# Attention into an ELU layer on one core: two tiles of tokens share each first product from tile 8 on, and the second products run some ten steps behind

## The chip, the cores and the metric

The kernel runs on one core of one Trainium2 chip. A core has a matrix engine (TensorE, PE in the profile), a vector engine (VectorE, DVE), a scalar engine (ScalarE, ACT), a GpSimd engine (POOL) and a sync engine (SP). Each has its own queue of instructions. SP, ACT and POOL also issue DMA transfers, which all run on the same 16 DMA engines. SBUF is the working memory, with 128 partitions; PSUM is the memory that TensorE writes, in eight banks of 128 partitions by 2 KB. The metric is the device time of one execution in microseconds (us), less being better.

## The reference

```python
def _attn_ref(q, k, v):                       # 8 batches, 8 heads, 576 positions, 64 numbers
    scores = scale * np.matmul(q, k.transpose(0, 1, 3, 2))
    mask = np.abs(pos[:, None] - pos[None, :]) <= 32
    scores = np.where(mask, scores, -1000000000.0)
    ...softmax over the last axis...
    return np.matmul(attn, v)

x = attn_out.transpose(0, 2, 1, 3).reshape(4608, 512)
h = x @ w_in                                  # 512 x 2048
g = np.where(h > 0.0, h, np.exp(np.minimum(h, 0.0)) - 1.0)
out = g @ w_out                               # 2048 x 512
```

So a sliding-window attention makes 4608 tokens of 512 numbers each, and a two-layer network with an ELU between its layers turns them into the output. All inputs and the output are float32.

## The kernel before

**Tokens.** The 4608 tokens are cut into 18 tiles of 256 tokens (`TT`), numbered t. Attention works on blocks of 64 positions and takes two blocks at a time, a pair i of 128 tokens; there are 36 pairs, and tile t consists of pairs 2t and 2t+1. A batch is nine blocks, that is four and a half pairs.

**Steps.** The network's work is cut into 144 steps, kk, in the order of the list `order`. A step is one tile and two of the sixteen 128-wide blocks of the inner layer (`FG` = 2), so a tile has eight steps. Steps 0 to 15 are those of tiles 0 and 1 mixed; from step 16 on tile t has steps 8t to 8t+7. In a step:

- `mm1` makes the first products of the step into a PSUM bank (`h0` and `h1` in turn): eight matmuls of a 128x128 block of `w_in` with 256 columns of `xT`, the tile's attention output turned to feature rows (L728).
- `exponents` takes the exponential of the bank on ACT (L738), `subtract` takes 1 from it on DVE (L750), and `elu` combines that with the bank on DVE into `g_sb` (L761). `elu` of step kk is queued in step kk+1. Since there are two banks, the first products of step kk+2 can start only when `elu` of step kk has read its bank.
- `mm2` adds the second products of step kk-2 (`LAG` = 2) to the tile's sums `psY` in PSUM banks `y0` and `y1`: four matmuls with 512 columns (L773). After a tile's last step ACT copies one half of the sums out and DVE the other (`y_sb`, L290 and L292), and SP issues two output DMAs of 256 KB. The next tile's sums start in the same two banks.

**Attention between the steps.** The rest is put at steps by hand: `at(kk, slot, fn, ...)` queues a call at a slot of step kk. Within a step come, in this order, `elu` of the step before, the slot "dve", the first products with their exponential and subtraction, the slot "mid", the second products with their copies, and the slot "end". `begin[i]` is the step at which pair i starts, and both pairs of a tile start together: scores of both (L384) at "mid" of step S = `begin[i]`, exponentials `pu` of 1024 columns on ACT at S and S+1 (L395), masks `pm` on DVE at S+1 and S+2 (L404), the products with v at the end of S+2 (L416), and `normalize` into `x_st` on DVE at S+3 and S+4 (L425, L428). From pair 10 on `x_dma` then turns `x_st` into `xT` by a transposing DMA from SP (L455), at the ends of S+3 and S+4. `x_st` has two buffers, so that a pair's `normalize` waits for the transposing DMA of the pair two before it.

**Loading a batch.** For batches 3 to 7, q and k are loaded in float32 by four DMAs of 576 KB from SP (`load_qk`, L132, at step `l_qk`), cast in six parts to bf16 (`cast_qk`), written as rows to DRAM from the ACT queue (`write_rows`, L319), and read back by two transposing DMAs from SP (`transpose_rows`, L324). v is loaded by five DMAs from POOL (`load_v`, L151, from step `l_v`), and a copy of it shifted by 64 rows is made, on DVE (`rotate_v`, L175) or for batches 2 and 3 by DMA from SP (`rotate_v_dma`, L183). The steps of all this are in the table `{2: (0, 0, 0), 3: (15, 24, 22), ...}` at L642, whose third number is where the casts may begin.

The instructions of each engine run in the order in which the program makes these calls. The functions that the change touches, with the lines of the profile:

Of the kernel before, what the change touches and what calls it, by code (L numbers as in the profile page):

```python
# [21 lines left out]
def kernel(  # L22
# [100 lines left out]
    def load_qk(b, which, part, engs=(nc.sync, nc.sync)):  # L123
        z, nj = part
        mj = max(nj, HJ)
        t = lpool.tile([128, 2, mj * D], FP32, tag=f"f{which}{mj}",
                       name=f"f{which}", bufs=2 if part is WHOLE else 1)
        qk_f[b, which, z] = t
        src = (q, k)[which][b, :, z:z + NC * nj, :].rearrange(
            "(g h) (c j) d -> c g h (j d)", h=2, j=nj)  # L130
        for h in range(2):
            engs[h].dma_start(out=t[:, h, 0:nj * D], in_=src[:, :, h, :])  # L132
# [161 lines left out]
    def cast_qk(b, which, part, j0, n, eng, hs=slice(0, 2)):  # L294
        z, nj = part
        if (b, which, z) not in qk_b:
            qk_b[b, which, z] = lpool.tile(
                [128, max(nj, HJ), 2 * D], BF16,
                tag=f"b{which}{max(nj, HJ)}", name="qkb",
                bufs=2 if part is WHOLE else 1)  # L300
        t = qk_b[b, which, z]
        copy_on(eng,
                t[:, j0:j0 + n, :].rearrange("p j (h d) -> p h j d",
                                             h=2)[:, hs],
                qk_f[b, which, z][:, hs, j0 * D:(j0 + n) * D].rearrange(
                    "p h (j d) -> p h j d", d=D))
# [136 lines left out]

    def xT_of(i):
        t, z = i // 2, i % 2
        if z == 0:
            xT[t] = xpool.tile([128, 2, NDO, 128], BF16, tag="xT", name="xT")
        return xT[t][:, z, :, :]
# [168 lines left out]
    begin = {4: 9, 5: 12, 6: 18, 8: 26, 10: 31, 12: 37}  # L617
    for i in range(FIRST_TWO, NPAIR):
        begin[i] = begin.get(i - i % 2, STEPS * (i // 2) - 14)
# [15 lines left out]
    at(BACK_AT, "dve", swap_back)  # L635
    starts = set(begin.values())
    starts |= {begin[i] + 1 for i in range(FIRST_TWO, NPAIR)}
    for b in range(2, B):
# [3 lines left out]
        l_qk, l_v, c0 = {2: (0, 0, 0), 3: (15, 24, 22), 4: (35, 36, 41),  # L642
                         5: (52, 52, 57), 6: (68, 68, 73),
                         7: (84, 84, 89)}[b]
# [7 lines left out]
        if b <= 3:  # L652

            if b == 2:
                at(k0, "dve", rotate_v, b, 0, 1)
            at((21, 28)[b - 2], "mid", rotate_v_dma, b, 3 - b)
        else:
            for n, back in enumerate((10, 8, 3, 2)):
                m0 = 2 * (n // 2)
                at(k0 - back, "dve", rotate_v, b, m0, m0 + 2, (n % 2,))  # L660
# [12 lines left out]
        for n, (which, j0) in enumerate(  # L673
# [3 lines left out]
            if j0 == 12:  # L677
                at(free[n], "end", write_rows, b, which)
                at(free[n] + (3 if free[n] == 29 else 4), "mid",
                   transpose_rows, b, which)  # L680

    order = [(z, n + m) for n in range(0, HALF, 2) for z in range(2)
             for m in range(2)]
    order += [(z, n) for n in range(HALF, STEPS) for z in range(2)]
    order += [(t, n) for t in range(2, NT) for n in range(STEPS)]
    psH, e_t, m_t, g_t, psY = {}, {}, {}, {}, {}

    def mm1(kk):  # L690
        t, s = order[kk]
        if kk == BY_PAIRS[1]:
            return
        ks = BY_PAIRS if kk == BY_PAIRS[0] else (kk,)
        tags = ((f"h{kk % 2}", "s") if kk == NSTEP - 1 else
                ("s",) if kk == 2 else ("u",) if kk == 3 else (f"h{kk % 2}",))
# [6 lines left out]
        for p in range(len(ks)):  # L703
            for k in ks:
                for z in range(len(tags)):
                    products(k, z, p if len(ks) > 1 else None)
                if p == len(ks) - 1:
                    for z in range(len(tags)):
                        exponents(k, z)
                        if k == NSTEP - 1:  # L710
                            elu(k, z)
# [4 lines left out]
    def products(kk, z, pair):  # L716
        t, s = order[kk]
        ps = psH[kk][z]
        w = ps.shape[1]
        for j in range(w):  # L720
# [32 lines left out]
    def elu(kk, z=0):  # L753
        if z == 0:
            g_t[kk] = mpool.tile([128, FG, TT], BF16, tag="g_sb", name="g_sb",
                                   bufs=6)
# [10 lines left out]
    def sums_to(kk, ts, j, c):  # L767
        t, s = order[kk]
        to, cs = psY[t][ts], slice(0, D_MODEL)
        if c is not None:  # L770
            cs = slice(c * D_MODEL // 2, (c + 1) * D_MODEL // 2)
            to = psY[t][ts + c][:, 0:D_MODEL // 2]
        nc.tensor.matmul(  # L773
            to,
            lhsT=g_t[kk][:, j, ts * 128:(ts + 1) * 128],
            rhs=w_out_sb[:, s * FG + j, cs],
            start=(s == 0 and j == 0),
            stop=(s == STEPS - 1 and j == FG - 1))

    def rows_out(ts, c, eng):  # L780
        t = NT - 1
        if c is None:
            src, cs = psY[t][ts], slice(0, D_MODEL)
        else:
            cs = slice(c * D_MODEL // 2, (c + 1) * D_MODEL // 2)
            src = psY[t][ts + c][:, 0:D_MODEL // 2]
        y_sb = opool.tile([128, D_MODEL], FP32,
                          tag=f"y_sb{int(eng is nc.vector)}", name="y_sb")
        copy_on(eng, y_sb[:, cs], src)
        (nc.scalar if c == 1 else nc.sync).dma_start(  # L790
            out_t[t, :, ts, cs], y_sb[:, cs])

    def mm2(kk, parts=((0, 0), (0, 1), (1, 0), (1, 1))):
        t, s = order[kk]
        if s == 0:
            psY[t] = [ps_tile([128, D_MODEL], FP32, g, "psY")
                      for g in (("h2", "t0") if t == 1 else ("y0", "y1"))]
            if t == NT - 1:
                psY[t].append(ps_tile([128, D_MODEL], FP32, "u", "psY"))
        last = t == NT - 1  # L800
        for ts, j in parts:

            for c in ((0, 1) if last and ts else (None,)):
                sums_to(kk, ts, j, c)
        if s == STEPS - 1 and not last:
            for ts in range(2):
                eng = (nc.scalar, nc.vector)[ts]
                y_sb = opool.tile([128, D_MODEL], FP32, tag=f"y_sb{ts}",
                                  name="y_sb")
                copy_on(eng, y_sb, psY[t][ts])  # L810
                nc.sync.dma_start(out_t[t, :, ts, :], y_sb)

    LAG = 2
    for kk in range(NSTEP + LAG):
        run(kk, "first")
        for n in {1: (), 2: (0, 1)}.get(kk, (kk - 1,) if kk < NSTEP else ()):
# [6 lines left out]

        for n in {2: (), 3: (), 4: (), 5: (0, 1), 6: (2, 3), 7: (4,), 8: (5, 6)}.get(
                kk, (kk - LAG,) if kk >= LAG else ()):

            if n < NSTEP - 2:
                run(kk, n)
                mm2(n)
            elif n == NSTEP - 1:  # L830
                for part in ((n - 1, 0, 0, None), (n - 1, 0, 1, None),
                             (n - 1, 1, 0, 0), (n - 1, 1, 0, 1),
                             (n, 0, 0, None), (n, 0, 1, None)):
                    sums_to(*part)
                rows_out(0, None, nc.scalar)
                for c in range(2):
                    for part in ((n - 1, 1, 1, c), (n, 1, 0, c),
                                 (n, 1, 1, c)):
                        sums_to(*part)
                    rows_out(1, c, (nc.vector, nc.scalar)[c])  # L840
        run(kk, "end")

# [29 lines left out]
```

## Time and profile before

| what | value |
|---|---|
| median of 3 runs | 303.7 us (303.46 to 304.2) |
| the profiled execution | 303.12 us |
| its span in the profile | 301.4 us, 7717 instructions |
| PE busy | 294.1 us, 98% |
| DVE busy | 240.9 us, 80% |
| ACT busy | 170.1 us, 56% |
| PE waits in total, by the list of waits | 3.3 us |
| DMA | 52.68 MB, 175 GB/s over the span |

The span is the time from the first to the last instruction in the profile; the execution lies 1.7 us above it. A busy time is that of an engine's instructions in the profile, and the matmuls' ends are modelled, so that PE is best read by the distance from one matmul's start to the next. A line such as `L728` is the source line that issued the instruction; helpers such as `copy_on` (L290, L292) stand for several uses. DMA-issuing instructions appear under SPq, ACTq and POOL.

### The profile page before, as it was taken

The numbers are of one execution on the slowest core, as the hardware profiler recorded it, in microseconds if no ns is written. First come the engines' busy times: TensorE is split into PE (matmuls) and PEld (weight loads), VectorE is DVE, ScalarE is ACT, GpSimd is POOL, SyncE is SP. The second block draws the span as 40 slices with busy tenths as digits, with TensorE's granted clock in tenths as the row PEclk, the third lists the DMA queues.
The fourth block names the chain that finished last, engine by engine and source line by source line (L and its number), as shares of the span: only waits on it lengthen the run. The fifth ranks groups of instructions, "written<-read, shape, count | busy, mean of one in ns | idle before, by whom it ended". The sixth has DMA issues, their size and how long they took to land.

```text
span 301.4 us, 7717 instructions
## 1 busy us (share of the span) xinstructions
PE 294.1 (98%) x3118; PEld 198.4 (66%) x3118; DVE 240.9 (80%) x479; ACT 170.1 (56%) x258; POOL 50.3 (17%) x72
## 2 busy tenths in 40 slices
PE   7999999999999999999999999999999999999994
PEld 3675667677666666666666666666666666666673
DVE  6778587988787988888888888877888787877663
ACT  3783558688655567456745674466535353533332
POOL 8857103620005000410032003200000000000000
PEclk9999999999999999999999999999999999999999
DMA  9999999999967948999899979997921111111012
GB/s 190 183 200 206 187 238 366 362 147 219 254 156 191 250 111 265 234 274 143 161 258 331 157 206 256 306 148 148 270 40 72 35 72 38 70 37 70 2 70 71
DMA packets 93157, 52.68 MB, mean 175 GB/s; under 512 B 77122, under 2 KB 83010, under 8 KB 93122
## 3 DMA queue, kind: packets, MB, share of 16 engines
q1 hardware_dynamic: 47330, 35.48, 44.3%
q0 software_dynamic: 43920, 10.10, 44.2%
q10 hardware_dynamic: 1872, 6.62, 6.4%
q8 instruction: 24, 0.39, 0.6%
q14 instruction: 11, 0.09, 0.1%
HBM read 36.70 MB, written 15.34 MB: 173 GB/s over the span
## 4 chain that ended last, share of the span: by engine, by line
PE 93%; DVE 2%; ACT 1%; DMA 1%; issue 1%; DVEq 0%; ACTq 0%
PE ps L728 42%; PE psY L773 41%; PE psS L416 4%; PE psS L384 3%; DMA f<-in_q_dram 1%; PE ptx L340 1%; PE psXT L438 1%; ACT pu L395 1%; PE ptx L335 1%; DVE qkb L292 1%; PE psS L364 1%; DVE x_st L428 0%; ACT qT L290 0%; PE ps_idle L479 0%; DVE pm L404 0%
## 5 line engine op out<-in xcount | busy, mean ns | idle before, releaser
L738 ACT ACTIVATE e_sb<-ps 128x512 f32<-128x512 f32 (+1 forms) x145 | 86.2, 595 | 114.9 <-PE ps L728 106.9
L728 PE MATMUL ps<-xT,w_in_sb 128*128 128x256 bf16 (+1 forms) x1168 | 149.2, 271 | 0.0
L773 PE MATMUL psY<-w_out_sb,g_sb 128*128 128x512 bf16 (+1 forms) x592 | 147.5, 374 | 0.0
L728 PEld LDWEIGHTS <-w_in_sb 128*128 128x128 bf16 x1168 | 110.8, 98 | 36.3 <-issue 0.5
L761 DVE SCALAR_TENSOR_TENSOR g_sb<-ps,m_sb 128x512 bf16<-128x512 f32 (+1 forms) x145 | 99.3, 686 | 13.1 <-DVE m_sb L750 0.5
L750 DVE TENSOR_SCALAR m_sb<-e_sb 128x512 bf16<-128x512 f32 (+1 forms) x142 | 61.5, 433 | 34.4 <-ACT e_sb L738 32.4
L773 PEld LDWEIGHTS <-g_sb 128*128 128x128 bf16 x592 | 56.1, 98 | 38.5 <-DVE g_sb L761 0.3
L151 POOL DMA_DIRECT2D Ve<-in_v_dram x37 | 31.7, 868 | 133.5 <-PE psS L416 79.9
L395 ACT ACTIVATE pu<-psS 128x1024 bf16<-128x1024 f32 x36 | 36.5, 1021 | 1.3 <-PE psS L384 1.3
L428 DVE TENSOR_TENSOR x_st<-psS,rc 128x512 bf16<-128x512 f32 x36 | 24.9, 691 | 1.2
L290 ACT CAST qkb<-f 128x768 bf16<-128x768 f32 (+1 forms) x29 | 25.0, 861 | 0.0
L404 DVE TENSOR_TENSOR pm<-pu,masks 128x1024 bf16<-128x1024 bf16 x32 | 21.8, 682 | 0.4 <-ACT pu L395 0.4
L416 PEld LDWEIGHTS <-pm 128*64 128x64 bf16 x512 | 9.7, 110 | 7.4 <-DVE pm L404 6.1
L292 DVE COPY y_sb<-psY 128x512 f32<-128x512 f32 (+1 forms) x18 | 12.1, 670 | 1.1 <-PE psY L773 1.1
L384 PEld LDWEIGHTS <-kT 64*128 64x128 bf16 x560 | 9.3, 95 | 4.4 <-issue 4.0
L290 ACT COPY y_sb<-psY 128x512 f32<-128x512 f32 (+1 forms) x19 | 10.9, 572 | 1.7 <-PE psY L773 1.7
L416 PE MATMUL psS<-Ve,pm 128*64 128x65 bf16 x288 | 11.6, 196 | 0.1
L384 PE MATMUL psS<-qT,kT 64*128 64x64 bf16 x560 | 11.5, 191 | 0.1
L416 PE MATMUL psS<-Vo,pm 128*64 128x65 bf16 x224 | 10.3, 196 | 0.0
L175 DVE COPY Vo<-Ve 64x1040 bf16<-64x1040 bf16 (+1 forms) x22 | 9.1, 414 | 0.7
L290 ACT COPY qT<-ptx 128x1152 bf16<-128x1152 bf16 (+4 forms) x9 | 7.7, 881 | 3.4 <-PE ptx L340 2.5
L425 DVE RECIPROCAL rc<-psS 128x8 f32<-128x8 f32 x36 | 7.2, 199 | 0.9 <-PE psS L416 0.9
(54 smaller groups left out, 88.2 us busy)
## 6 DMA issues: line engine op xcount, KB each, us to landing
out_dram<-y_sb SPq DMA_DIRECT2D x35, 256.0 KB, 3.3
f<-in_q_dram SPq DMA_DIRECT2D x12, 576.0 KB, 6.3
f<-in_k_dram SPq DMA_DIRECT2D x12, 576.0 KB, 8.3
in_dram<-qkb ACTq DMA_DIRECT2D x10, 576.0 KB, 4.3
Ve<-in_v_dram POOLq DMA_DIRECT2D x21, 128.0 KB, 12.6
w_in_sb<-in_moe_w_in_dram POOLq DMA_DIRECT2D x3, 512.0 KB, 10.1
w_out_sb<-in_moe_w_out_dram POOLq DMA_DIRECT2D x3, 512.0 KB, 10.9
Ve<-in_v_dram POOLq DMA_DIRECT2D x14, 96.0 KB, 11.5
```

What stands on the lines that cost most here:

```text
L151: nc.gpsimd.dma_start(out=V_e[b % 3][p0:p1, m, :, 0:D], in_=v[b, :, lo + p0:lo + p1, :].rearrange("h p d -> p h d"))
L290: nc.scalar.copy(d_, s_)
L384: nc.tensor.matmul(psS[:, h % 2, hp * 128 + z * QB:hp * 128 + (z + 1) * QB], lhsT=keys, rhs=qT[b % 2][base:base + 64, hp, QB * qb:QB * (qb ...
L395: nc.scalar.activation(pu, _bap(psS, [psS.ap[0], [1, 1024]]), AX.Exp, scale=SCALE)
L404: nc.vector.tensor_mul(pm, pu, _bap(mm, [mm.ap[0], [0, H], [1, 2 * QB]]))
L416: nc.tensor.matmul(psS[QB * z:QB * (z + 1), par, hp * VD:(hp + 1) * VD], lhsT=pm[:, par * HP + hp, z * QB:(z + 1) * QB], rhs=vv[:, qb // 2 ...
L428: nc.vector.tensor_mul(x_st, _bap(psS, [psS.ap[0], [VD, HP], [512, 2], [1, D]]), _bap(rc, [rc.ap[0], [2, HP], [1, 2], [0, D]]))
L728: nc.tensor.matmul(o, lhsT=w_in_sb[:, do, fo * 128:(fo + 1) * 128], rhs=r, start=(do == 0), stop=(do == NDO - 1))
L738: nc.scalar.activation(e_sb, ps, AX.Exp)
L750: nc.vector.tensor_scalar(m_sb, e_sb, -1.0, None, ALU.add)
L761: nc.vector.scalar_tensor_tensor(g_t[kk][:, z * w:(z + 1) * w, :], ps, 0.0, m_t.pop((kk, z)), ALU.max, ALU.min)
L773: nc.tensor.matmul(to, lhsT=g_t[kk][:, j, ts * 128:(ts + 1) * 128], rhs=w_out_sb[:, s * FG + j, cs], start=(s == 0 and j == 0), stop=(s == ...
```

## The change

From tile 8 on the tiles are taken two at a time. `xT` then holds four pairs, and a step is one 128-wide block of the inner layer for both tiles: four matmuls of 512 columns instead of eight of 256, into one bank as before. The exponential, the subtraction and `elu` keep their shapes. There are still 144 steps, of which steps 64 to 143 are of the new kind; tiles 8 and 9 share steps 64 to 79, and so on.

From step 18 on the second products are no longer bound to a step. `todo` lists those of tiles 2 to 16 in order, and each step takes four of them from its head (`more_sums`), or three in the steps of the set `light` as long as fewer than 48 are outstanding beyond two steps' lag, and it stops after the last one of a tile. `light` holds, for each start S, the steps S, S+5, S+6 and S+7, without those that write rows to DRAM. The number that is outstanding grows from 12 at step 18 to 48 at step 89. `g_sb` gets 23 buffers instead of 6 for this. The last tile's sums all run after the loop (`last_sums`): its first half, then 384 and at last 128 columns of its second half.

The starts move: pairs 16 and up begin two steps earlier than before. The loads of q and k of batches 4 to 7 move from steps 35, 52, 68 and 84 to 33, 50, 66 and 82, those of v from 36, 52, 68 and 84 to the same steps, and the casts' first steps by two. Batch 4's shifted v is now made by DMA, at step 41. The buffers `f` and `qkb` have one size now, shared by halves and whole loads, two of each. `xT` has four buffers for single tiles and two for double ones, instead of five.

```diff
     def load_qk(b, which, part, engs=(nc.sync, nc.sync)):
         z, nj = part
-        mj = max(nj, HJ)
-        t = lpool.tile([128, 2, mj * D], FP32, tag=f"f{which}{mj}",
-                       name=f"f{which}", bufs=2 if part is WHOLE else 1)
+        t = lpool.tile([128, 2, SJ * D], FP32, tag=f"f{which}",
+                       name=f"f{which}")
...
+    WIDE = 8
+
     def xT_of(i):
-        t, z = i // 2, i % 2
+        n = 2 if i < 2 * WIDE else 4
+        t, z = i // n * n // 2, i % n
         if z == 0:
-            xT[t] = xpool.tile([128, 2, NDO, 128], BF16, tag="xT", name="xT")
+            xT[t] = xpool.tile([128, n, NDO, 128], BF16, tag=f"xT{n}",
+                               name="xT", bufs=4 if n == 2 else 2)
...
-    begin = {4: 9, 5: 12, 6: 18, 8: 26, 10: 31, 12: 37}
+    begin = {4: 9, 5: 12, 6: 18, 8: 26, 10: 31, 12: 37, 14: 42}
     for i in range(FIRST_TWO, NPAIR):
-        begin[i] = begin.get(i - i % 2, STEPS * (i // 2) - 14)
+        begin[i] = begin.get(i - i % 2, STEPS * (i // 2) - 14 - 2 * (i >= 2 * WIDE))
...
-        l_qk, l_v, c0 = {2: (0, 0, 0), 3: (15, 24, 22), 4: (35, 36, 41),
-                         5: (52, 52, 57), 6: (68, 68, 73),
-                         7: (84, 84, 89)}[b]
+        l_qk, l_v, c0 = {2: (0, 0, 0), 3: (15, 24, 22), 4: (33, 33, 39),
+                         5: (50, 50, 55), 6: (66, 66, 71),
+                         7: (82, 82, 87)}[b]
...
-        if b <= 3:
+        if b <= 4:
 
             if b == 2:
                 at(k0, "dve", rotate_v, b, 0, 1)
-            at((21, 28)[b - 2], "mid", rotate_v_dma, b, 3 - b)
+            at((21, 28, 41)[b - 2], "mid", rotate_v_dma, b, int(b == 2))
...
-    order += [(t, n) for t in range(2, NT) for n in range(STEPS)]
+    order += [(t, n) for t in range(2, WIDE) for n in range(STEPS)]
+    made = {(t, n * FG + j): (kk, j * TT)
+            for kk, (t, n) in enumerate(order) for j in range(FG)}
+    for t in range(WIDE, NT, 2):
+        for fo in range(NFO):
+            for z in range(2):
+                made[t + z, fo] = len(order), z * TT
+            order.append((t, fo))
...
     def products(kk, z, pair):
...
+        if t >= WIDE:
+            for do in range(NDO):
+                nc.tensor.matmul(
+                    _bap(ps, [ps.ap[0], [128, 4], [1, 128]]),
+                    lhsT=w_in_sb[:, do, s * 128:(s + 1) * 128],
+                    rhs=xT[t][:, :, do, :],
+                    start=(do == 0), stop=(do == NDO - 1))
+            return
...
+    todo = [(t, n * FG + j, ts) for t in range(2, NT - 1)
+            for n in range(STEPS) for ts in range(2) for j in range(FG)]
+    light = {begin[i] + n for i in range(FIRST_TWO, NPAIR)
+             for n in (0, 5, 6, 7)} - writes
+    LEAD = 10 * 2 * FG
+
+    def more_sums(kk):
+        behind = (kk + 1 - STEPS * 2) * 2 * FG - (576 - 64 - 32 - len(todo))
+        n = 3 if kk in light and behind < LEAD + 8 else 4
+        left = len(todo) % (NFO * 2) or NFO * 2
+        if left <= n + 1:
+            n = left
+        while todo and n:
+            t, fo, ts = todo[0]
+            if made[t, fo][0] > kk - LAG:
+                break
+            todo.pop(0)
+            if fo == 0 and ts == 0:
+                begin_sums(t)
+            sums_to(t, fo, ts)
+            n -= 1
+            if fo == NFO - 1 and ts == 1:
+                for ts in range(2):
+                    rows_out(t, ts)
+                break
+
+    def last_sums():
+        t = NT - 1
+        begin_sums(t)
+        for ts, c, eng, queue in ((0, 0, nc.scalar, nc.sync),
+                                  (1, 1, nc.vector, nc.sync),
+                                  (1, 2, nc.vector, nc.scalar)):
+            for fo in range(NFO):
+                sums_to(t, fo, ts, c)
+            rows_out(t, ts, c, eng, queue)
...
+    while kk <= NSTEP or todo:
...
+        if kk >= 2 * STEPS + LAG:
+            more_sums(kk)
...
+    last_sums()
```

`sums_to` adds one second product, `begin_sums` takes the banks of a tile's sums, and `rows_out` copies a half out and issues its DMA; `made` gives the step and the place at which a block of `g_sb` was made.

## The prediction

> **What bounds the kernel now.** I read the page's busy times first, then the list of waits, then the timeline of a late stretch. The page gives PE 98%:
>
> ```profile
> PE 294.1 (98%) x3118; PEld 198.4 (66%) x3118; DVE 240.9 (80%) x479; ACT 170.1 (56%) x258; POOL 50.3 (17%) x72
> ```
>
> From 46 us on, the list of PE's waits is empty. The timeline of 285 to 301.4 us shows a plain step:
>
> ```profile
> 288.63 1.04 PE L728 MATMUL ps<-xT,w_in_sb 128*128 128x256 bf16 x8
> ...
> 289.71 0.60 ACT L738 ACTIVATE e_sb<-ps 128x512 f32<-128x512 f32 x1 [1.15 <-PE ps L728]
> ...
> 290.33 0.43 DVE L750 TENSOR_SCALAR m_sb<-e_sb 128x512 bf16<-128x512 f32 x1 [0.52 <-ACT e_sb L738]
> 290.37 1.04 PE L728 MATMUL ps<-xT,w_in_sb 128*128 128x256 bf16 x8
> 290.87 0.69 DVE L761 SCALAR_TENSOR_TENSOR g_sb<-ps,m_sb 128x512 bf16<-128x512 f32 x1
> ```
>
> First, a step is 1.738 us from start to start: eight first products at 109.2 ns and four second products at 216. PE streams without a gap. Second, the chain first products, exponential, subtraction, `elu` ends at 290.87 + 0.69 = 291.56, 2.93 us after its step began. The step after next needs that bank 3.48 us after, so the slack is 0.55 us less some 0.05 for the semaphore. Steps with scores or products with v are 0.68 and 0.73 us longer and lend slack.
>
> Then the transfers. SP's timeline around batch 4's loads:
>
> ```profile
> 83.30 2.26 SPq L324 DMA_TRANSPOSE kT<-in_dram  x1
> 86.95 1.43 SPq L811 DMA_DIRECT2D out_dram<-y_sb  x2
> 88.98 3.27 SPq L455 DMA_TRANSPOSE xT<-x_st  x2
> 92.30 1.27 SPq L132 DMA_DIRECT2D f<-in_q_dram  x2
> 93.62 1.33 SPq L132 DMA_DIRECT2D f<-in_k_dram  x2
> ```
>
> Pairs 10 and 11 are transposed at 88.98 and 91.06, ahead of batch 4's loads. The same operation just behind batch 5's loads, and then all from 205 us on, by the transfers of `xT`:
>
> ```profile
> DMA to landing us min/median/max: 8.6/8.8/9.0
> ...
> DMA to landing us min/median/max: 2.4/2.4/4.8
> ```
>
> Behind loads a transposition takes 9 us instead of 2.4.
>
> **What the Trainium skill says.** "TensorE: Matmul & The Clock Gate", section "Wait — 56ns, not 53.3ns?": a warm matmul takes N/2.4 ns plus 2.5; the trace agrees (109.2 and 216). Its section "Back-to-back issue gap" has 131 ns for sustained 512-column matmuls; the trace says 216 and decides. The same page, Part 2, says that matmuls stay in program order and only weight loads are pulled ahead: PE can't pass a waiting product. Its Part 1 says that about 3.4 us of an idle window halves the clock; no stage of this trace idles so long before the end. "DMA: Bandwidth & Descriptors", "HWDGE ordering": SP's transfers share one ring on each DMA engine, read in order; the 9 against 2.4 us agree.
>
> **The change part by part.** *Shared products.* 640 matmuls of 256 columns become 320 of 512: 320 x (218.4 - 215.8) = -0.8 us. The halved weight loads save nothing, being 98 ns under slots of 109 already. Bounds: 0 to -1.0.
>
> *The end.* Now the last output waits for SP, busy with the other half: from the last sum's end (297.60) to the last landing (300.45) 2.85 us. Afterwards only 128 columns remain: copy about 0.29 (512 columns take 0.68 on DVE, 256 take 0.42), landing 2.25 (the ACT queue's now), gaps 0.07, so 2.6; and 0.1 us of waits on `elu` between the last sums goes. Together -0.34. The sums themselves are equal, 16 x (216 + 2 x 109.2) against 16 x (216 + 162.5 + 56).
>
> *Light steps.* Three second products instead of four make a plain step 1.52 us. That isn't saved, but owed: 11 such steps before step 40 (18, 23, 25, 26, 31, 32, 33, 35 to 38) are 2.38 us to be done later. But two in a row leave 3.04 us for a chain of 2.93, so whatever else stands on DVE or ACT there now stops PE. I went through the queues step by step with the rows' durations, for both kernels. For before this gives PE 0.1 us of waits after step 16, as the trace does. The places afterwards:
> - Step 35 is light and now ends tile 3: pair 11's `normalize` (0.9) and a sum's copy (0.6 net) stand ahead of `elu`, which ends 3.6 us after the step's start against 3.04. PE loses 0.6 in all.
> - Step 45 has two second products only (tile 4 ends), 1.31 us, with `normalize`, both copies and ACT's casts (0.83 each) at steps 44 to 46. PE loses 0.17 + 0.17 in steps 46 and 47 and 0.46 at step 48.
> - Step 81 is light, ends tile 8, and ACT has pair 25's 1.02 us exponential ahead of its copy. That copy ends 1.67 + 0.92 + 0.48 = 3.07 us after the step's start. The next tile's first sum, at 1.51 + 0.86 = 2.37, needs that bank: 0.74.
> - Small ones: 0.17 each before the products with v of pairs 11 and 15, 0.13 at step 56, 0.05 elsewhere, and 0.25 in steps 24 to 31.
>
> After step 40 these are 0.17 + 0.17 + 0.17 + 0.46 + 0.13 + 0.74 + 0.05 = 1.9, less 0.05 that before has at step 95: +1.8. Those ahead of step 40 vanish in the next item.
>
> *Batch 4's loads.* At step 33 they stand on SP right behind batch 3's last row transposition, and now ahead of pairs 10 and 11, which are tile 5, wanted at step 40. Before, that row transposition was issued at 83.30 and took 2.26; with 0.73 us gained in steps 18 to 28, 82.57. So the loads start at 84.8. The four loads took 11.2 us from first issue to last landing before (92.30 to 103.5), and for the other batches 10.3, 11.1 and 10.3; mean 10.7: 95.5. In the ring follow pair 10, tile 3's two outputs (512 KB, ready at 90.7) and pair 11, beside v's transfers, whose start moves as well. In the trace these four landed 5.7, 7.7, 5.0 and 8.1 us after the loads; the last of them is now pair 11. Mean 6.6: 102.1, between 100.1 and 104.1. Step 40 could start at 99.22 - 2.38 + 0.75 = 97.6. PE idles about 4.6 us, 2.5 to 6.5, with `mm1` at the head of its queue and the second products behind it; DVE and ACT run dry with it. Step 40 starts 2.9 us later than before. Bounds: not at all, if loads don't delay transpositions, to +5.
>
> *Other late x.* An odd tile's second pair now has four steps from S+4 to its use, 6.5 to 6.9 us, where before it had ten. In the trace it landed 6.7, 4.6, 6.9, 4.5 and 4.5 us after the start of that step. So 0.2 to 0.3 at step 64, about nothing at 80 and 96: +0.25, bounds 0 and 1.5.
>
> *At nothing.* Batch 4's shifted v by DMA takes four copies of 0.43 from DVE and puts 520 KB on SP's ring ahead of pair 13 (4.5 to 5.3 us in the trace): lands near 110 us, wanted near 116. Without that cover it would be a second stop. Batch 3's loads wait for batch 1's casts through the shared buffers, some 1.5 us, seven steps ahead of use. `g_sb`'s 23 buffers exceed the 19 steps for which one is held.
>
> Sum on the span: 2.9 + 2.4 + 1.8 + 0.25 - 0.8 - 0.34 = +6.2, 301.4 to 307.6; the execution 303.1 to 309.3; the median of the runs, 0.6 above it, 303.7 to 309.9.
>
> **Rivals.** *Queue waits alone*: tile 5 arrives in time, since loads and transposition overlap on the 16 engines. Then all queue waits count: 2.8 + 0.25 - 0.15 - 1.14 = +1.8, 305.5. Against it are four batches of 9 us landings in the trace. *The clock falls*: if PE idles a whole 3.4 us window at step 40, its clock halves, and at least 3.4 us of matmuls at half speed cost 1.7 more: 311.6 to 313. In the trace the granted clock is 1.00 to 299 us and 0.98 in the last 2.4, so it falls about 3.7 us after the last sum; 4.6 us of idling may or may not hold such a window. *The lead covers it* (other side): if PE could go on with second products while a first product waits, the 23 outstanding at step 40 (5.0 us) would fill the hole, and the other waits too: -1.14, 302.6. It decides from 6.2 us of covered waits on; program order speaks against it. *Sharing doesn't do what it says*: PE is streaming already, so 0.8 us is all; at 131 ns a matmul it would be 27 us, which the 216 ns of the second products deny.
>
> **How the numbers follow.** Main case 0.63 (306.5 to 311.5), queue waits alone 0.13, the clock 0.14, the lead 0.06, none of these 0.04. The likeliest gives 309.9. The range, from queue waits alone to a fallen clock, is 305.0 to 312.5. About 0.3% (0.9 us) is what a measurement here can tell from no change: faster 0.07, same 0.03, slower 0.90.
>
> **What would show it.** Right: a hole of 2.5 to 6.5 us on PE just before step 40, near 97 to 102 us, waiting for `xT` by DMA; pair 11's transposition taking 9 us or more; shorter waits near steps 37, 46 to 48 and 82; from step 96 on, steps of 1.727 us. Wrong: pair 11 landing by 97.5 us, PE's waits unchanged in total, or a different hole, such as one at step 48 behind batch 4's shifted v or at steps 64, 80 or 96, where odd tiles arrive last.

## The result and the profile after

The changed kernel takes 312.14 us (311.06 to 313.56) against 303.45 for the one before: a ratio of 1.0285, 95% interval 1.0254 to 1.0316. The profiled execution took 312.55 us, with a span of 310.8, 9.4 more than before. The forecast was 309.9; the result lies within its range, near the upper end, and in the band of the rival in which the clock falls.

The page of the changed kernel gives PE 95% instead of 98%. PEclk is the clock granted to TensorE in 40 slices of the span:

```profile
PE 295.1 (95%) x2757; PEld 167.8 (54%) x2798; DVE 238.6 (77%) x474; ACT 169.6 (55%) x256; POOL 50.0 (16%) x72
...
PEclk9999999999999799999999999999999999999999
```

PE isn't busier in microseconds (295.1 against 294.1), so most of the time is in what it waits for. And the clock has one digit of 7, in the 14th slice, from 101 to 109 us; before it had none. All six executions of the changed kernel were granted 0.994 or 0.989 of the clock on average, so each of them has a fall like this one. The changed kernel's list of PE's waits (in total, times, longest), which was empty from 46 us on:

```profile
PE ps L747 <- DMA xT<-x_st: 3.1, 1, 3.1
...
PE psY L798 <- ACT y_sb L289: 1.3, 2, 0.8
```

The one wait for `xT` is at step 40. The timeline of PE around it (start, duration, engine; in brackets the idle time before and what ended it):

```profile
101.95 1.66 PE L747 MATMUL ps<-xT,w_in_sb 128*128 128x256 bf16 x8 [3.09 <-DMA xT<-x_st]
103.83 1.49 PE L798 MATMUL psY<-w_out_sb,g_sb 128*128 128x512 bf16 x3 [0.22 <-issue]
105.11 1.29 PE L747 MATMUL ps<-xT,w_in_sb 128*128 128x256 bf16 x8
106.23 1.03 PE L798 MATMUL psY<-w_out_sb,g_sb 128*128 128x512 bf16 x4
```

Two things stand here. PE stops for 3.1 us with tile 5's first product at the head of its queue. Then eight first products take 1.66 us instead of 1.04, and of the second products a start-to-start distance of 427 ns instead of 216: half the clock. (The records lack 40 of the 592 second products, so that the x3 and its wait of 0.22 stand for four.) Matmul by matmul, the first two after the stop are still at 109 ns, the doubling begins at about 102.2 us and ends at 105.6, 3.4 us later. SP's timeline tells why tile 5 is late:

```profile
85.89 1.26 SPq L131 DMA_DIRECT2D f<-in_q_dram  x2
87.20 1.25 SPq L131 DMA_DIRECT2D f<-in_k_dram  x2
88.95 1.32 SPq L457 DMA_TRANSPOSE xT<-x_st  x1
91.05 1.26 SPq L811 DMA_DIRECT2D out_dram<-y_sb  x2
92.36 9.16 SPq L457 DMA_TRANSPOSE xT<-x_st  x2
```

Pairs 10 and 11 are now issued behind batch 4's loads; pair 11, issued at 92.36, landed at 101.82. The answer of the trace for the transpositions of pairs 10, 11 and 12 gives, from issue to landing (the shortest is pair 12's, issued at 100.33, when batch 4's q and k were in):

```profile
DMA to landing us min/median/max: 6.2/9.5/10.0
```

Where the 9.4 us went, by stretches of steps (step starts of both traces):

| stretch | before, us | after, us | difference | of which |
|---|---|---|---|---|
| start to step 14, nothing changed in it | 43.50 | 44.38 | +0.88 | ten idle matmuls of the warm-up all at the slow clock; 43.5 to 44.4 in the traces of all runs below |
| steps 14 to 38 | 53.13 | 51.94 | -1.19 | 11 second products put off, -2.38; waits +1.2 |
| steps 39 to 41 | 6.08 | 10.78 | +4.70 | the stop 3.03, the clock 1.67 |
| steps 42 to 142 | 191.15 | 188.97 | -2.18 | 25 products put off, -5.40; sharing, -0.8; waits +4.0 |
| step 143 to the end | 7.52 | 14.72 | +7.20 | 36 products made up, +7.78; the end, -0.58 |

What is put off comes back to the last product. The loss is the stop, the clock, 5.2 us of small waits and 0.9 at the start, less 1.4 for sharing and the end.

### The profile page after: what moved, and what is told of

Same layout as the page of the kernel before. It is cut to its first block, busy times and chain, and to the rows that moved or that the text cites. A ratio compares the mean times of both kernels' runs of the same rounds, so it can differ in the third digit from the quotient of the medians.

```text
span 310.8 us, 7035 instructions
## 1 busy us (share of the span) xinstructions
PE 295.1 (95%) x2757; PEld 167.8 (54%) x2798; DVE 238.6 (77%) x474; ACT 169.6 (55%) x256; POOL 50.0 (16%) x72
## 4 chain that ended last, share of the span: by engine, by line
PE 83%; DVE 6%; DMA 5%; issue 3%; ACT 3%; SPq 0%; DVEq 0%; ACTq 0%
PE psY L798 35%; PE ps L733 22%; PE ps L747 15%; PE psS L413 3%; PE psS L381 3%; DMA xT<-x_st 3%; DVE g_sb L780 2%; DMA f<-in_k_dram 2%; ACT pu L392 1%; PE ptx L337 1%; DVE x_st L425 1%; DVE m_sb L769 1%; PE psXT L435 1%; DVE pm L401 1%; PE ptx L332 1%
## 5 line engine op out<-in xcount | busy, mean ns | idle before, releaser
L757 ACT ACTIVATE e_sb<-ps 128x512 f32<-128x512 f32 x144 | 86.0, 598 | 114.3 <-PE ps L733 66.6
L798 PE MATMUL psY<-w_out_sb,g_sb 128*128 128x512 bf16 (+2 forms) x552 | 141.2, 374 | 5.1 <-issue 2.3
L780 DVE SCALAR_TENSOR_TENSOR g_sb<-ps,m_sb 128x512 bf16<-128x512 f32 x144 | 99.2, 690 | 12.7 <-ACT m_sb L767 0.5
L769 DVE TENSOR_SCALAR m_sb<-e_sb 128x512 bf16<-128x512 f32 x141 | 60.3, 428 | 40.6 <-ACT e_sb L757 39.0
L733 PE MATMUL ps<-xT,w_in_sb 128*128 128x512 bf16 x320 | 82.2, 379 | 0.2
L747 PE MATMUL ps<-xT,w_in_sb 128*128 128x256 bf16 (+1 forms) x528 | 67.1, 272 | 3.6 <-DMA xT<-x_st 3.1
L747 PEld LDWEIGHTS <-w_in_sb 128*128 128x128 bf16 x528 | 49.0, 99 | 20.0 <-issue 4.6
L733 PEld LDWEIGHTS <-w_in_sb 128*128 128x128 bf16 x320 | 30.5, 98 | 37.3 <-issue 1.6
L291 DVE COPY y_sb<-psY 128x512 f32<-128x512 f32 (+2 forms) x19 | 12.5, 657 | 7.6 <-PE psY L798 7.6
L289 ACT COPY y_sb<-psY 128x512 f32<-128x512 f32 x18 | 10.5, 583 | 5.7 <-PE psY L798 5.7
L413 PE MATMUL psS<-Vo,pm 128*64 128x65 bf16 x224 | 11.2, 197 | 0.0
```

Of the source, the lines that this page charges most:

```text
L289: nc.scalar.copy(d_, s_)
L413: nc.tensor.matmul(psS[QB * z:QB * (z + 1), par, hp * VD:(hp + 1) * VD], lhsT=pm[:, par * HP + hp, z * QB:(z + 1) * QB], rhs=vv[:, qb // 2 ...
L733: nc.tensor.matmul(_bap(ps, [ps.ap[0], [128, 4], [1, 128]]), lhsT=w_in_sb[:, do, s * 128:(s + 1) * 128], rhs=xT[t][:, :, do, :], start=(do ...
L747: nc.tensor.matmul(o, lhsT=w_in_sb[:, do, fo * 128:(fo + 1) * 128], rhs=r, start=(do == 0), stop=(do == NDO - 1))
L757: nc.scalar.activation(e_sb, ps, AX.Exp)
L769: nc.vector.tensor_scalar(m_sb, e_sb, -1.0, None, ALU.add)
```

## The experiments

**Batch 4's loads behind pairs 10 and 11.** This undoes one entry of the table of steps:

```diff
-        ... 4: (33, 33, 39),
+        ... 4: (35, 36, 41),
```

> The changed kernel with one edit: batch 4's loads of q and k go back to step 35, of v to step 36, its casts to step 41, so that pairs 10 and 11 are transposed ahead of them. Theory (the loads delay tile 5, and the idling lowers the clock): PE's wait for xT at step 40 (3.2 us) goes, the granted clock stays at 1.00 until the end, which the changed kernel's trace puts at another 1.67 us; 312.1 - 4.8 = 307.3 us. Rival A (the delay comes from v's transfers and tile 3's outputs, or from the starts moved in other ways): the wait stays over 2 us and the time is 311 or more. Rival B (the hole only moves: later casts and rows for batch 4 bring a stop before step 56, where batch 4 is first used): the wait at 40 goes and a new one of over 2 us stands near step 56, 309 to 311 us.

Measured: 321.2 us, ratio 1.054 (1.048 to 1.060). PE's wait for `xT` is gone and the clock from 100 to 120 us is 1.00, as the theory has it; but it is rival B that decides the time, on a larger scale than it said. The longest of PE's waits in this kernel:

```profile
PE psS L381 <- DMA kT<-in_dram: 12.0, 1, 12.0
```

SP's timeline of this kernel ahead of that wait:

```profile
119.05 1.66 SPq L131 DMA_DIRECT2D f<-in_q_dram  x2
120.77 2.38 SPq L131 DMA_DIRECT2D f<-in_k_dram  x2
123.37 4.28 SPq L457 DMA_TRANSPOSE xT<-x_st  x2
128.27 9.31 SPq L321 DMA_TRANSPOSE kT<-in_dram  x1
```

With casts two steps later, batch 4's k rows are turned at step 54, behind batch 5's loads of step 50, and its first scores at step 56 wait 12 us; the clock is at half for 13.7 us from 134.7 on. A smaller stop, of 2.0 us at step 48, comes from `x_st`, whose `normalize` waits 1.7 us for a transposition. The entries of the table hang together: with batch 5's loads at 50, casts of batch 4 that begin at 41 bring its k rows behind them. This entry could not be taken back alone.

**Idle matmuls in the hole.** Step 40 as late as before, but PE kept busy:

```diff
+        if kk == 40:
+            idle(14, "h0")
         if kk < NSTEP:
             mm1(kk)
```

> The changed kernel with 14 idle matmuls of 512 columns (14 x 0.216 = 3.0 us) queued just ahead of step 40's first products, into the bank that these will use; the late transposition stays. Theory (idling is what halves the clock): step 40 starts within 0.3 us of where it started (102), PE is busy in the place of its wait, the clock stays at 1.00 and 1.7 us come back: 310.4. Rival (the clock falls for another reason, such as the load on the chip): steps 40 and 41 stay 1.4 and 0.25 us too long, 312.1.

Measured: 309.96 us, ratio 1.0203 (1.0175 to 1.023), 2.2 below the changed kernel. PE's timeline:

```profile
98.39 3.19 PE L481 MATMUL ps_idle<-zeros 128*128 128x512 bf16 x14
101.64 1.03 PE L747 MATMUL ps<-xT,w_in_sb 128*128 128x256 bf16 x8
102.51 1.03 PE L798 MATMUL psY<-w_out_sb,g_sb 128*128 128x512 bf16 x4
```

Step 40 starts as late as it did (101.64), and at full speed. So idling is what lowers the clock. In the traces steps 39 to 41 are 1.59 us shorter than the changed kernel's, which fits the 1.67 of the table, and steps 42 to 142 another 1.13: there PE's wait at step 73 is gone, since ACT's cast of step 71 waits 0.62 us for its load instead of 1.49, of which more below.

**The light steps elsewhere.** The same lead built with two products instead of four in the long steps S and S+2:

```diff
-             for n in (0, 5, 6, 7)} - writes
-    LEAD = 10 * 2 * FG
+             for n in (0, 2)}
+    LEAD = 44
...
-        n = 3 if kk in light and behind < LEAD + 8 else 4
         left = len(todo) % (NFO * 2) or NFO * 2
+        n = 2 if kk in light and behind < LEAD and left > 4 else 4
```

> The changed kernel with its light steps elsewhere: two second products instead of four in the steps S (scores) and S+2 (products with v) alone, which are 0.68 and 0.73 us longer than a plain step, until 44 are outstanding; loads as changed. Theory (short steps in a row expose DVE's and ACT's queues): the waits of 0.17 to 0.93 us at steps 45 to 48, 54 to 56, 66 to 73, 82 and 86 to 90, some 4 us together, fall to under 1; 14 products instead of 11 are owed at step 40, which starts at the same 102 us, so 0.65 is given back: 312.1 - 3 + 0.65 = 309.7. Rival (the waits are not due to short steps but to the casts, copies and masks themselves, and reappear in other steps): 311.5 or more.

Measured: 312.3 us, ratio 1.029 (1.023 to 1.036): the rival's number. The waits at steps 45 to 48, 69 to 73 and 86 to 87 did go. Others came: with 44 outstanding a tile ends in S+1, where ACT has an exponential of 1.02 us ahead of its copy, 0.5 us in each of seven tiles; the products with v of S+2 reach PE before their masks, 1.1 us in three places. And the stop at step 40, of 3.5 us, cost more of the clock: granted 0.83 on average from 100 to 120 us, where the changed kernel has 0.91. This is the slowest of the four executions, 315.2 us; two of the others were granted the full clock throughout and took 310.8 and 311.4, still above the theory's 309.7.

**Loads back, casts late, light steps in long steps, all at once.** The edits of the first and third experiments, and:

```diff
-        ... 5: (50, 50, 55), 6: (66, 66, 71), 7: (82, 82, 87)
+        ... 5: (50, 50, 57), 6: (66, 66, 73), 7: (82, 82, 89)
```

> Three edits at once on the changed kernel: batch 4's loads behind pairs 10 and 11 (35, 36, casts 41), the light steps in S and S+2, and the casts of batches 5 to 7 two steps later (57, 73, 89, seven steps after their loads). If the losses are those read from the trace and add up: 312.1 - 3.2 (wait at 40) - 1.7 (clock) - 2.4 (owed products: nothing is idled away any more) + 0 - 3.5 (waits of the queues) is 301.3 at the least; with 0.9 of the start, which differed between the two traces before any changed step, 302.2; and 303.5 if a third of the waits stays. Rival (lead and shared steps bring waits of their own wherever they are put): 305 or more.

Measured: 343.05 us, ratio 1.131. It fell into the first experiment's trap three times: waits for `kT` of 18.4 us in all, at steps 56, 72 and 88. Another stop, of 5.7 us at step 47, has its cause in `x_st`, whose `normalize` waits 5.9 us for a transposition, and the clock is at half for 30.7 us in all. It tells nothing on the sum of the losses, only that the order of SP's queue outweighs everything else here.

**The loads back, with the rest of the queue in order.** Only q and k of batch 4 move back; v stays at 33, and a line not shown keeps the light steps where they were:

```diff
-        ... 4: (33, 33, 39), 5: (50, 50, 55), ...
+        ... 4: (35, 33, 41), 5: (51, 51, 57), ...
-            at((21, 28, 41)[b - 2], "mid", rotate_v_dma, ...
+            at((21, 28, 44)[b - 2], "mid", rotate_v_dma, ...
-        free = [f for f in range(c0, k0) if f not in starts]
+        free = [f for f in range(c0, k0)
+                if f not in starts or (b, f) == (4, 48)]
...
-                at(free[n] + (3 if free[n] == 29 else 4), "mid",
+                at(free[n] + (3 if free[n] in (29, 48, 63) else 4), "mid",
```

> The changed kernel with the loads of batch 4's q and k behind pairs 10 and 11 (step 35; v stays at 33), and this time nothing else late through it: batch 4's casts at 41, 44 to 48 and its k rows turned at 51, batch 5's loads at 51 behind them, batch 5's casts from 58, batch 4's shifted v at 44. The light steps are the same ones. Theory (q's and k's loads delay pair 11, and the idling halves the clock): PE's wait for xT at step 40 falls from 3.2 us to under 0.5, the clock stays at 1.00, the 2.2 to 3 us of queue waits stay: 312.1 - 3.2 - 1.7 = 307.3. Rival A (v's loads and tile 3's outputs, which are still ahead of pair 11, make the delay): a wait of 2 us or more stays, 310 or more. Rival B (tile 5 would in any case have come no earlier than step 42 or so): the wait is 1 to 2.5 us without a fall of the clock, 308.5 to 310.

Measured: 310.2 us, ratio 1.0224 (1.0201 to 1.0248). Pair 11 landed at 97.5 us, 5.5 after its issue; steps 39 to 41 took 5.95 us against 10.78, and the clock stayed at 1.00. So q's and k's loads made the stop, not v's, which are where they were. The sum was missed by 2.9 us, mostly because of two new waits: 0.7 at step 50, behind the cast that I put on ACT at step 48, and 2.0 at step 61. DVE's timeline there:

```profile
140.38 0.69 DVE L425 TENSOR_TENSOR x_st<-psS,rc 128x512 bf16<-128x512 f32 x1 [2.08 <-DMA xT<-x_st]
```

And PE's, with the next step's first products:

```profile
142.26 1.03 PE L748 MATMUL ps<-xT,w_in_sb 128*128 128x256 bf16 x8 [1.83 <-DVE g_sb L781]
```

Batch 5's loads of step 51 stand ahead of pair 17's transposition, which takes 11.9 us. `x_st` has two buffers, so the `normalize` two pairs later waits for it on DVE, and `elu` and PE behind that. A transposition behind loads is thus late twice: for the tile that it makes, and for the buffer that it holds.

**The part with the early loads alone, on the kernel before.**

```diff
-        ... 4: (35, 36, 41),
+        ... 4: (33, 33, 41),
```

> The kernel before with one part of the change alone: batch 4's loads of q, k and v at step 33 instead of 35 and 36; casts, light steps and the rest as before. Theory: the loads start about 85.6 us, are in by 97, and pair 11's transposition lands 5 us after them, near 102.3, where step 40 could start at 99.2: a wait of 3 us at step 40, and 1.7 more if the clock halves: 306.5 to 308.3. Then the light steps add nothing to this stop; they only arrive at it 2.4 us earlier. Rival (without light steps PE's lead covers it): under 1 us, 304.3 or less.

Measured: 309.96 us, ratio 1.0214 (1.0191 to 1.0238). One row of the table costs 6.3 us. PE's timeline:

```profile
104.22 1.87 PE L728 MATMUL ps<-xT,w_in_sb 128*128 128x256 bf16 x8 [4.73 <-DMA xT<-x_st]
```

The stop is longer than expected because tile 3's outputs, at step 33 in this kernel, stand ahead of the loads, which start at 88.50 instead of 85.89. Pair 11 lands 15.6 us after the first load is issued; in the changed kernel it was 15.9. The clock takes another 2.0. In the changed kernel the same stop begins with 11 products put off, so that step 40 starts only 2.7 us later than before; that is not a saving, since these are made up at the end.

**The lead alone.** There are no shared products, and loads, starts and casts are as before; only the light steps, 23 buffers of `g_sb` and the last tile apart remain:

```diff
-    WIDE = 8
+    WIDE = 18
```

> One part of the change alone: second products behind, with the changed kernel's light steps (S, S+5, S+6, S+7, one product fewer each), 23 buffers of g_sb and the last tile apart; no shared products, no earlier starts, loads, casts and batch 4's shifted v as before. Theory (short steps expose DVE's and ACT's queues): 1.5 to 4 us of waits of 0.1 to 1 us each, at steps 35 to 37, 45 to 50 and wherever a tile ends in a light step, less 0.5 for the end: 304.7 to 307.2, with the clock at 1.00 and no wait over 1.5 us. Rival (the lead costs nothing without the earlier loads and starts): 303.0 to 303.5.

Measured: 308.1 us, ratio 1.0134 (1.0081 to 1.0187), slower than I expected; the profiled execution has 305.5 of span, 4.2 more than before, and in the list of waits none of PE's is longer than 0.6 us after the first microseconds. PE's timeline at steps 45 to 48:

```profile
107.82 1.05 PE L747 MATMUL ps<-xT,w_in_sb 128*128 128x256 bf16 x8
...
109.14 1.04 PE L747 MATMUL ps<-xT,w_in_sb 128*128 128x256 bf16 x8
...
111.22 1.05 PE L747 MATMUL ps<-xT,w_in_sb 128*128 128x256 bf16 x8
...
113.30 0.93 PE L747 MATMUL ps<-xT,w_in_sb 128*128 128x256 bf16 x7 [0.38 <-DVE g_sb L780]
```

Steps of 1.32, 2.08 and 2.08 us with two, four and three second products: 5.48 us, where before took 5.22 for twelve. A short step is followed by long ones, because DVE's and ACT's work doesn't shrink with it. Over all steps, 36 products (7.78 us) are put off, and the steps become shorter by only 2.73. The other 5.05 us are waits. This is as large a loss as the stop and the clock together (4.70), and PE's rows in the list of waits show only a part of it (1.1 us for `elu`): a matmul's modelled end lies 0.16 us behind the next one's possible start, so that a wait counts only beyond it, and what a weight load waits for, which PE pulls ahead, counts as PEld's.

**All three repaired together, and its twin with narrow products.** The loads as in the experiment that put them back, light steps in S and S+2 with 48 outstanding, casts of batches 6 and 7 at 73 and 89; the twin makes each shared product as two of 256 columns:

```diff
+            for z in range(2):
+                for do in range(NDO):
+                    nc.tensor.matmul(
+                        _bap(ps, [ps.ap[0], [128, 2], [1, 128]], z * 256),
+                        lhsT=w_in_sb[:, do, s * 128:(s + 1) * 128],
+                        rhs=xT[t][:, 2 * z:2 * z + 2, do, :],
+                        start=(do == 0), stop=(do == NDO - 1))
```

> The same order of loads, and in addition the light steps as two second products in S and S+2 (48 outstanding, so that a tile ends in S+2 from step 82 on, not in S+1), and the casts of batches 6 and 7 two steps later. The shared products, the lead and the last tile apart remain. If the losses are the late tile, the clock and the waits of the queues, and nothing else: before's 303.5, less 0.8 for sharing and 0.5 for the end, plus at most 1 us of waits that remain: 302.2 to 303.2, within 0.5% of before. Rival (the lead or the sharing costs something that no wait shows): 304.5 or more.

> The same kernel with the shared steps' four products of 512 columns made as eight of 256, the same numbers into the same bank. Theory (320 x 2 x 109.2 against 320 x 215.8 ns): 0.8 us above the one with wide products, steps of 1.738 instead of 1.727 us from step 91 on. Rival (halving the weight loads matters[...]): more than 3 us above it.

Measured: 310.2 us, ratio 1.0214 (1.0172 to 1.0256), and for the twin 310.9, ratio 1.0200 (1.0158 to 1.0241). Single runs of each lie up to 4.6 and 7.7 us apart, so the two times can't tell 0.8 us; the steps can. From step 130 to 143, where nothing waits, a step takes 1.7267 us with wide products and 1.7367 with narrow ones: 10.0 ns a step, 0.80 us over 80 steps, and nothing like the rival's 3.

The first expectation failed. The stop and the fall of the clock are gone, but PE's waits in this kernel hold

```profile
PE ps L734 <- DVE g_sb L781: 3.1, 2, 1.7
PE psS L413 <- DVE pm L401: 2.0, 4, 0.9
```

The first two are at steps 76 and 92, where `normalize` waits for `x_st` as above; the others are products with v that come before their masks, one of them behind the cast at step 48. The steps from 14 to 143 are as long as before's to 0.04 us, with 8.6 us of products taken out of them.

**The lead in S alone.** This changes the kernel with all three repaired: the steps S go without any second product (n = 0; eight of them do, the rest are at the end of a tile or past the lead), `x_st` has four buffers and `g_sb` 21, batch 4's last cast goes from ACT at 48 to DVE at 47, and batch 5's loads stand at 50:

```diff
-             for n in (0, 2)}
+             for n in (0,)}
...
-        n = 2 if kk in light and behind < LEAD and left > 4 else 4
+        n = 0 if kk in light and behind < LEAD and left > 4 else 4
-        x_st = apool.tile([128, H, D], BF16, tag="x_st")
+        x_st = apool.tile([128, H, D], BF16, tag="x_st", bufs=4)
```

> The kernel with loads back, casts late and the lead built in long steps, with four more edits: the lead is built in S alone (no second products there at all in nine steps, so that the products with v in S+2 do not come early); x_st has four buffers instead of two, so that a normalize no longer waits for a transposition that stands behind loads (g_sb 21 buffers to make room); batch 4's last cast goes to DVE at step 47, not to ACT at 48; batch 5's loads at 50. Theory (what is left above before in that kernel are three kinds of waits: products with v for their masks in S+2, 2.0 us; normalize for x_st at steps 76 and 92, 3.9 us; the cast at 48, 1.1 us): these go, one of 0.5 at step 81 stays, and the span falls from 308.9 to about 302.4, the time to 304. Rival (each wait taken away makes room for another one, since the chain's slack is 0.55 us a step and the lead brings the products forward everywhere): 306.5 or more.

Measured: 305.3 us, ratio 1.0053 (1.0038 to 1.0069). The waits named did go, and with all these edits together 6.9 us of the changed kernel's 8.7 are gone. Still 3.1 us of the 8.6 put off or saved are lost in waits, most of it at steps 19, 20, 31, 36, 47, 63, 66 and 82 (the last 0.7). The time lies midway between theory and rival, and it isn't enough to pass the kernel before.

**The end alone, on the kernel before.** The last tile's second half as 384 and 128 columns, the last 128 columns of all sixteen blocks summed at the very end:

```diff
-            cs = slice(c * D_MODEL // 2, (c + 1) * D_MODEL // 2)
+            cs = (slice(0, 384), slice(384, D_MODEL))[c]
...
-            for c in ((0, 1) if last and ts else (None,)):
+            for c in ((0,) if last and ts else (None,)):
...
+                rows_out(1, 0, nc.vector)
+                for k in range(NSTEP - STEPS, NSTEP):
+                    for j in range(FG):
+                        sums_to(k, 1, j, 1)
+                rows_out(1, 1, nc.vector)
```

> The kernel before with its end alone changed: the second half of the last tile's sums is cut 384 and 128 columns instead of 256 and 256, the last 128 columns of all sixteen blocks are summed after everything else (16 x 56 ns), both are copied on DVE, and g_sb has 11 buffers. From the last sum's start to the span's end before takes 4.02 us and the changed kernel 3.48. Theory: that 0.5 us is had without any lead: 303.5 - 0.5 = 303.0, a ratio of 0.998. Rival (16 short matmuls at the end cost more than they save, or wait for the last elu): 303.5 or more.

Measured: 303.29 us against 303.64, ratio 0.9982 (0.9970 to 0.9994). Of the parts tried alone on the kernel before, this is the only one that pays, and this kernel is the only one here that is faster than the one before, by 0.35 us, less than three runs can tell from none. Sharing and the earlier starts were not tried alone on it. In its trace the time from the last sum's start to the span's end is 3.10 us against 4.05 before; by the medians most of these 0.95 us is taken back ahead of it, where the short matmuls stand.

## Why the prediction was right or wrong

**Batch 4's loads: right, with errors that cancelled.** Pair 11 was forecast to land at 102.1 and landed at 101.82; step 40 started 2.7 us later than before, forecast 2.9. On the way the loads started 1.1 us later than forecast (85.89, most of it the late start), took 11.5 us instead of 10.7, and pair 11 came 4.5 us after them instead of 6.6. The 6.6 came from batches whose outputs entered SP's queue only when the loads were nearly in (at 133.78, with the last load in at 134.06); here they were issued from 91.05 on, 6.3 us before that. The step rested on the Trainium skill, "DMA: Bandwidth & Descriptors", section "Queues, rings and completion order", paragraph "HWDGE ordering", by which each DMA engine reads one ring of SP's transfers in order; the traces agree: pair 11 took 9.5 us behind the loads, 5.5 ahead of them.

**The clock: this is the step that failed.** The main case left the fall of the clock out, and the rival that had it asked for a whole window of 3.4 us without work, so that "may or may not hold such a window" got 0.14. A wait of 3.1 us was enough, less than the 4.6 that the forecast itself had. The term that was put at nothing is 1.67 us, and the filled hole takes it away.

What I hadn't used is in Part 1 of "TensorE: Matmul & The Clock Gate" of the Trainium skill: its window of about 3.4 us runs freely, so that a stop can fall anywhere in it. The traces fit that. Wherever a stop of PE was followed by a fall, the clock stayed at half for 3.41 us or for two, three or four times that. The lines below give a stretch, its length, the busy time of PE, PEld, DVE, ACT and POOL, and the granted clock; the last two numbers are DMA's. This is the changed kernel's stretch just before its clock fell:

```profile
98.78:102.20 3.42, 0.33 (x9) 0.26 (x4) 1.48 (x3) 0.00 (x0) 0.00 (x0) 1.00 1.82 194
```

And this is the twin with narrow products, whose clock fell after a stop of 2.02 us, at step 76:

```profile
167.74:171.16 3.42, 1.40 (x10) 0.72 (x9) 1.85 (x5) 1.36 (x3) 0.00 (x0) 1.00 0.93 251
171.16:174.57 3.41, 3.41 (x14) 1.81 (x13) 2.67 (x5) 1.32 (x2) 0.00 (x0) 0.50 0.91 204
```

So a stretch need not be wholly idle, as the prediction took Part 1 to say: PE worked in it for 0.33 us in the one kernel and for 1.40 in the other. Stops of 1.98 us (loads behind pairs 10 and 11, step 48) and of 1.83 us (loads back, step 61) left the clock at 1.00. In these traces the limit is thus near 2 us of idling. That it counts where the stop lies would explain why the same kernel with long light steps kept its clock in two of four executions; that isn't shown, since only one of the four was traced.

**Light steps: the debt right, the waits half.** 36 products put off came back as 7.8 us, and those of steps 14 to 38 vanished in the stop as forecast (2.38 less 1.2 of waits). Of the waits after step 40, every one that was named is in the trace at its size: steps 46 and 47 are 0.34 and 0.44 us longer than their products take (0.80 forecast around them), step 82 0.73 (0.74 forecast). But 2.2 us more came where I had named none, in two kinds. In steps 69 to 71, 86 and 87 (0.9 us) DVE's copies for the shifted v (L174, 0.42 us) stand in light steps, and at step 66 0.2. And at steps 73 and 90 (1.2 us) ACT's cast waits for its load. ACT's timeline of the changed kernel, then PE's:

```profile
164.34 0.83 ACT L289 CAST qkb<-f 128x768 bf16<-128x768 f32 x1 [1.49 <-DMA f<-in_q_dram]
165.08 0.59 ACT L757 ACTIVATE e_sb<-ps 128x512 f32<-128x512 f32 x1
165.56 1.02 ACT L392 ACTIVATE pu<-psS 128x1024 bf16<-128x1024 f32 x1
166.47 0.59 ACT L289 COPY y_sb<-psY 128x512 f32<-128x512 f32 x1
```

```profile
167.11 1.02 PE L798 MATMUL psY<-w_out_sb,g_sb 128*128 128x512 bf16 x4 [0.77 <-ACT y_sb L289]
```

Loads and casts both moved by two steps, so the forecast gave them no cost and no line. But on SP the loads wait for the row transposition of the batch before, which moved less. Before, batch 6's q was issued in step 69, four steps ahead of its cast at the end of step 73; now it is in step 68, three ahead of step 71, and behind the cast stand an exponential, a `pu` and the copy that frees the bank. With the filled hole the same q was issued in step 67, the cast waited 0.62 us, and PE's wait at step 73 was not there.

**Late x at 64, 80 and 96: none.** Forecast 0.25. Tile 9's second pair landed at 146.4, before step 64 at 147.9.

**Sharing: right.** -0.8 forecast; 10.0 ns a step, -0.80, by the twin kernels. The halved weight loads gave nothing, as said.

**The end: right in kind, small in size.** -0.34 forecast, -0.58 measured by the stretches, of which 0.54 after the start of the last sum.

**The sum.** 6.2 forecast, + 1.7 for the clock, + 2.2 for the waits not named, - 0.25 for late x, - 0.2 for the end, - 0.2 for step 40, makes 9.4. The start's 0.88 is within that, since the forecast set step 40 by pair 11's landing.

**The rivals.** Queue waits alone: denied, the loads did delay tile 5. The clock: its fall is there, and 312.1 lies in its band of 311.6 to 313. That it lies there is in part luck: the trace has 2.2 us of waits that the rival did not contain, against 0.65 of small terms that were smaller than forecast, and the median lay 0.4 us below the profiled execution instead of 0.6 above. The lead covers it: denied, PE stood at the first product with 23 second products outstanding. Sharing that doesn't do what it says: denied by the twin. With the loads in order and the clock up, the lead alone would still have cost 4 us in the span: the sign of the forecast did not hang on step 40.

## What to carry to other kernels

Work put off is not work saved: count what comes back, and count for every step that becomes shorter whether the chain through the other engines becomes shorter too; here 36 products put off bought 2.7 us of 7.8. When a load moves ahead of a transfer in the same queue, ask what that transfer makes and which buffer it holds, and look for all row transpositions, loads and casts that must keep their order with it. A stop of the matrix engine of 2 us or more must be priced with the clock (1.67 us here after a stop of 3.1, 2.0 after one of 4.7), and can be filled with idle matmuls to see that price.

## What was not expected of the hardware

In the changed kernel the clock fell not during the stop but 0.3 us after PE had resumed, and it stayed at half for 3.4 us. After stops of 3.5 us (light steps elsewhere) and 4.7 us (early loads alone) it fell during the stop and stayed at half for 6.8 us in both kernels, and it could fall after a stop of only 2.0 us. Before step 14, where all kernels have the same work in the steps, their traces differ by up to 0.9 us (43.5 to 44.4), which is as much as many of the single effects studied; differences of that size were therefore read from the distances between steps. And the transposing DMAs of `xT` that were issued within 3 us behind four loads took 8.3 to 13.1 us in every kernel that had one, whatever else was moved.
